# Filler matmuls ahead of the first weights in eight blocks instead of one, and a newly laid out issue table

## The chip, the core and the metric

The kernel runs on one core of one Trainium2 chip. A core has five engines that run side by side, each through its own list in order, and wait for one another by semaphores: TensorE (PE in the profile; PEld are its weight loads), VectorE (DVE), ScalarE (ACT), GpSimd (POOL) and SyncE (SP). SP here does nothing but issue DMAs; a few are issued by ACT. The metric is the device time of one execution in microseconds (us), median of the runs.

## The reference, cut to what matters

One block of a transformer with conditioning, on 2048 tokens of 512 features (bf16):

```python
mod = silu(c) @ w_mod                      # six rows of 512: sa, ca, ga, sb, cb, gb
h = layernorm(x) * (1 + ca) + sa
x = x + ga * A(h)                          # attention over 8 tokens, spaced by 2, 32 heads of 16
h = layernorm(x) * (1 + cb) + sb
x = x + gb * B(h)                          # second layernorm, then an MLP over the tokens
```

A: `qkv = h @ wqkv`; each token attends to itself and to the tokens 2, 4, ... 14 before it; then `@ wo`. B mixes tokens, not features: `gelu(h.T @ w1 + b1) @ w2 + b2` with w1 of 2048 x 1792 and w2 of 1792 x 2048.

## The kernel before, in words

The 2048 tokens are 16 tiles of 128. `SIZES=(2, 4, 4, 4, 2)` groups the tiles into five chunks, and `build_chunk(ch)` adds the work of one chunk to a graph. Names in the table carry the chunk or the tile.

Of one chunk: `ln1s`, `ln1v`, `rstd1`, `rste1`, `nb1`, `n1` are the first layernorm of its tiles (statistics, variance, an Ln and an Exp on ACT, the norm). `tr` transposes the normed tiles on PE and `hT` evicts them with the scale `a1col`; for chunks 2 to 4, `xt` does the transposing by DMA. `qkv{ch}_{t}{j}` are the projections (t: 0 q, 1 k, 2 v), `ev` their evictions from PSUM. `halo_v` copies the last 16 tokens of the chunk before, `vd` are four DMAs that lay v out anew. `qk` (VectorE, four of 128x4096 a chunk, or 128x2048 in the short chunks 0 and 4) multiplies q by the shifted k's, `red` sums the products over the head on PE; `max`, `sub`, `exp`, `esum`, `rcp`, `rcq`, `smB` are the softmax; the four `a2` DMAs lay its weights out for `pv` (VectorE, as large as `qk`), whose products `pvacc` sums on PE and `oev` evicts. `wo` is the output projection, `x1` adds the result to x, `ln2*` and `ln3*` are the layernorms of B with `n2`, `aff`, `afb`, `h3`. Chunks 0 and 1 use the raw weights, and the scale goes into `hT`; the others use weights that `wsc` has scaled.

The MLP: `mlp1_{layer}_{ft}_{tile}` are the first matmuls over those token tiles that are normed already, `park` and `padd` hold partial sums, `gelu` closes them; `mlp2_{tile}` are fourteen matmuls of 512 columns for each output tile, `fin` and `st_out` finish and store.

The opening: `ld_c`, then `cps` (a tiny matmul that transposes c), `silu_exp`, `silu_dve`; `modcols1` and `modcols0` are 16 small matmuls each on the loads `ld_wmod1` and `ld_wmod0`, and give `a1col` (1 + ca) and `sab` (sa). `qvb0` and `qvb1` project sa through the raw weights. `warm` blocks are fillers: matmuls of 512 columns on the identity into a PSUM buffer that nobody reads.

What sets the order: nothing is moved at run time. `ORDER` (line 180) is one list of all operations. `_Graph.schedule` (line 87) walks it, checks that everything an operation needs stands ahead of it, picks the engine, and gives out ring buffers (six PSUM banks, four product buffers `big`, five `vd` buffers) in that order; each engine's list is the table's order. A suffix picks the engine where several can do the work (`:a` ACT, `:d` VectorE, `:p` GpSimd, none the first one named in the code); `:s` skips, and `:q` splits a matmul into four of 32 columns of weights. SP's DMAs are such a list too: a DMA that waits holds all behind it.

In the old table PE's list opens `cps tr0_0 warm0 modcols1 modcols0 tr1_2 tr1_0 qvb0 qkv0_00 qkv0_02 qkv0_10`. `warm0` has 12 matmuls, and the key `wmA1` makes both `modcols` wait for it (lines 538 and 553); `warm1` (2) stands at the end of the table, and the other six are skipped. All instructions have one line number in the profile, that of a helper, so rows are told apart by their tiles: psS<-ident is a filler, psS<-sc,big is `modcols`, psS<-ident,h a transpose, psS<-sab,wst is `qvb0`, psS<-hT,wst are projections, big<-q_sb,k_f is `qk`, big<-a2sb,vD is `pv`, lsb<-lsb,rb is `smB`, hT<-h on SP is `xt`.

Of the kernel before, what the change touches and what calls it, by code (L numbers as in the profile page):

```python
# [42 lines left out]
class _Graph:  # L43
# [7 lines left out]
    def add(self, eng, dur, fn, **kw):  # L51
        return self.add_any([(eng, dur, fn)], **kw)
# [103 lines left out]
def _ap(base, dims):  # L156
    return bass.AP(base.tensor, base.offset, [list(base.ap[0])] + [list(d) for d in dims])
# [23 lines left out]
halo0 ident ld_c act_table cps silu_exp ld_x1 ld_x0 ln1s0 ln1v0 ln1s1:a ln1v1 rstd1_0 rste1_0 ld_x_2_8 ld_x_1_2 nb1_0  # L181
consts ln1s9 silu_dve n1_1 n1_0:p tr0_0 ln1s8 ld_x_1_4 ln1s4:a ld_x_2_6 ln1s3:a warm0 ln1s5 ln1s7 ld_wmod1 ln1v5
ld_wmod0 modcols1 modcols0 ln1v9 ln1v8 ln1v4 ln1s2 ln1v2 ld_wqkv0 ln1v7 ln1v3 ln1s6 ln1v6 rstd1_1 rste1_1 nb1_1 n1_4:d
rstd1_2 rste1_2 n1_2:d n1_5:d nb1_2 ld_wqkv1 n1_3 n1_7 n1_6:d a1col hT0_2:d n1_9 tr1_2 tr1_0 hT1_1 wsc0_1:p hT0_1:d
sab hT0_0:d ld_x_3_12 hT0_3:d hT1_3:d qvb0 qvb_cp0 qkv0_00 warm6:s wsc1_3:a hT1_2:d qkv0_02 ev0_00 ld_wqkv2 qkv0_10
qkv0_12 ld_b2 ev0_10 ld_x_4_14 wsc1_2:p qkv0_20 wsc0_0 qvb1 ld_x_3_10 wsc0_3:p hT1_0:d ev0_02 wsc2_2:a ln1s13 ln1s12
ev0_12 ln1v12 ln1v13 wsc1_1:a qkv0_22 qk0_1 qkv1_13 ld_wmod2 ld_wo3 qk0_0 qk0_2 n1_8 red0_0 red0_1 ln1s11:a qkv1_03:q
qvb_cp1 qk0_3 xt6 red0_2 ld_wmod3 ev1_13 ev1_03 red0_3 mask wsc2_3:a ln1v11 ln1s10 ld_b1 ld_wo0 xt8 ev0_20 xt7 qkv1_11
ev1_11 ln1v10 max0 qkv1_01 ev1_01 rstd1_3 ev0_22 qk1_3 xt9 sub0 exp0 qkv1_00 ev1_00 qkv1_10 ev1_10 wsc1_0:a vd0_0
qk1_1 qkv1_02 esum0 rcp0 wsc0_2:p qk1_0 ev1_02 qkv1_12 qkv1_23 ld_wmod4 ld_wmod5 rcq0 ev1_12 qkv1_21 rste1_3 smB0  # L190
nb1_3 a2_0_0 ln1s15:a a2_0_2 qkv2_00 qk1_2 qkv2_10 n1_13:p red1_0 ev2_00 red1_1 ev2_10 red1_2 red1_3 ln1v15 a2_0_1
ev1_23 qkv2_13:q qk2_0 ev1_21 max1 modrow qkv1_20:q sub1:q ln1s14:a a2_0_3 pv0_0 wsc2_1:a halo_v1:a qkv1_22:q mrows
vd0_3 vd0_1 vd0_2 ld_wo1 ev2_13 pv0_3 pvacc0_0 n1_10 exp1 ev1_20 ld_row0 qkv2_02:q pv0_1 pv0_2 warm3:s ld_wo2 esum1:q
rcp1 ev1_22 rcq1 smB1 qkv2_03 ev2_03 pvacc0_1 pvacc0_2 xt10 wsc2_0:a pvacc0_3 ev2_02 oev0_2 qkv2_01:q vd1_3 qkv2_12
oev0_0 ev2_01 ln1v14 qkv2_11 ev2_12 rstd1_4 qkv2_23:q n1_11 vd1_1 n1_12 a2_1_2 qkv2_22:q a2_1_3 qk2_3 woq_s rste1_4
wo1:q wo0:q ev2_11 a2_1_0 a2_1_1 vd1_2 x1_1 red2_0 qk2_2 nb1_4 qk2_1 ev2_22 qkv2_20 x1_0 ev2_23 ln2m0 biascols pv1_3
n1_14 xt13 xt12 ln2q0 ln2q1 n1_15 qkv2_21 red2_1 red2_2 ln2w0 red2_3 xt11 rstd2_0 pv1_1 ev2_21 rste2_0 qkv3_10:q
ev3_10 qkv3_02:q ev3_02 qkv3_00:q ev2_20 ev3_00 nb2_0 n2_1 n2_0 qkv3_11 max2 qkv3_01 ev3_01 sub2 pvacc1_1 oev1_1
halo_v2 ld_row2 vd1_0 pvacc1_3 pv1_2 qkv3_12:q ld_row1 exp2 aff0 ev3_12 qkv3_13:q halo_v3:a ev3_11 pv1_0 esum2
pvacc1_2 rcp2 oev1_3 oev1_2 afb0 pvacc1_0 oev1_0 rcq2 xt14 ld_w1_0_0 ld_w1_0_512 vd2_2 qkv3_03:q qk3_1 smB2 ln3s0:a  # L200
# [38 lines left out]
def kernel(  # L239
# [27 lines left out]
    WARM=(12, 2, 2, 2, 2, 2, 2, 2),  # L267
# [28 lines left out]
    def ps(slot):  # L296
        return psS[slot.i][:]
# [731 lines left out]
```

## Time and profile before

| | |
|---|---|
| median of 3 runs | 198.6 us (197.77 to 198.84) |
| span of the profiled execution, first to last instruction | 196.8 us |
| the profiled execution's own time | not listed apart from the three runs; the median is 1.8 us over the span |
| PE busy | 185.2 us (94%), 1850 matmuls |
| VectorE busy | 156.6 us (80%), 244 instructions |
| ScalarE busy | 124.9 us (63%), 293 instructions |
| GpSimd busy | 19.9 us (10%), 38 instructions |
| DMA | 35.95 MB, mean 183 GB/s |

How to read it: times of the profile count from the first instruction. A matmul's recorded length includes its way through the array, so two in a row overlap in the record, and the spacing of their starts is the better measure; for that reason a busy PE is not PE at its peak. Idle time of an engine that is not the one that holds up the others costs nothing.

### The profile page before, as it was taken

The page shows a single profiled execution, that of the slowest core. Times are in us where ns is not written, and L with a number is a line of the kernel's source. Part 1 is how long each engine was busy: PE and PEld are TensorE (multiplying, and loading weights), DVE is VectorE, ACT ScalarE, POOL GpSimd, SP SyncE. Part 2 cuts the span into 40 slices and gives each one's busy share as a digit, 9 for nine tenths or more (in the row PEclk, how much of TensorE's full clock was granted, in tenths as well). Part 3 has the DMA queues.
Part 4 walks back from the last instruction along what each step waited for, and adds up shares of the span by engine and source line. Part 5 has one row for each costly group of instructions (what it writes and reads, how often), then busy time and mean ns, then how long its engine had stood idle before and what let it go on. Part 6 is the DMA issues. An engine that isn't in the chain of part 4 may idle for free.

```text
span 196.8 us, 4628 instructions
## 1 busy us (share of the span) xinstructions
PE 185.2 (94%) x1850; PEld 95.5 (48%) x1867; DVE 156.6 (80%) x244; ACT 124.9 (63%) x293; POOL 19.9 (10%) x38
## 2 busy tenths in 40 slices
PE   0699999999999999899999999999999999999994
PEld 0369554654444467244544454444444444444453
DVE  2888999999999999999999999965841633453664
ACT  6877999998999999999797889812760000000000
POOL 5123006320000005030000031200000000000000
PEclk9999999999999999999999999999999999999999
DMA  5998478778899732969674768888939293001112
GB/s 169 312 366 248 115 165 256 235 216 238 165 193 317 252 131 80 312 167 249 199 200 136 159 176 180 197 250 170 336 65 309 82 257 102 30 27 53 53 53 82
DMA packets 55369, 35.95 MB, mean 183 GB/s; under 512 B 24628, under 2 KB 52788, under 8 KB 55348
## 3 DMA queue, kind: packets, MB, share of 16 engines
q1 hardware_dynamic: 53468, 34.05, 63.2%
q10 hardware_dynamic: 1880, 1.61, 2.5%
q8 instruction: 14, 0.23, 0.5%
q14 instruction: 7, 0.06, 0.1%
HBM read 22.03 MB, written 2.10 MB: 123 GB/s over the span
## 4 chain that ended last, share of the span: by engine, by line
PE 73%; DVE 13%; ACT 5%; issue 3%; DMA 2%; SPq 1%; POOL 0%; DVEq 0%; ACTq 0%
PE psS L131 71%; DVE big L131 9%; DVE h L131 2%; PE psL L131 2%; ACT junk L131 1%; SPq L131 1%; DMA vD<-v_sb 1%; ACT xx L131 1%; DMA xx<-in_A_x_dram 1%; DVE m L131 1%; ACT o_sb L131 1%; ACT lsb L131 0%; DVE mv L131 0%; POOL h L131 0%; ACT v_sb L131 0%
## 5 line engine op out<-in xcount | busy, mean ns | idle before, releaser
L131 PEld LDWEIGHTS <-wst 128*128 128x128 bf16 (+1 forms) x566 | 35.5, 100 | 31.9 <-issue 1.3
L131 PE MATMUL psS<-h,wst 128*32 128x512 bf16 (+1 forms) x400 | 50.5, 379 | 0.4 <-issue 0.3
L131 DVE TENSOR_TENSOR big<-q_sb,k_f 128x4096 bf16<-128x4096 bf16 (+1 forms) x20 | 36.4, 1857 | 0.5 <-ACT k_f L131 0.5
L131 DVE TENSOR_TENSOR big<-a2sb,vD 128x4096 bf16<-128x4096 bf16 (+1 forms) x20 | 36.6, 1858 | 0.0
L131 DVE SCALAR_TENSOR_TENSOR h<-psS,bcol,rows_bc 128x512 f32<-128x512 f32 (+2 forms) x18 | 12.4, 690 | 24.2 <-PE psS L131 24.0
L131 PE MATMUL psS<-hT,w_qkv 128*32 128x512 bf16 (+3 forms) x414 | 28.7, 337 | 0.8 <-ACT v_sb L131 0.4
L131 PEld LDWEIGHTS <-w_qkv 128*32 128x32 bf16 (+1 forms) x462 | 19.9, 108 | 16.4 <-issue 2.7
L131 PE MATMUL psS<-gT,big 128*128 128x512 bf16 x109 | 24.3, 379 | 0.2
L131 POOL TENSOR_SCALAR h<-xx,rs,nb 128x512 bf16<-128x512 bf16 x6 | 10.6, 1777 | 84.2 <-DVE nb L131 84.2
L131 PEld LDWEIGHTS <-big 128*128 128x128 bf16 x144 | 12.0, 98 | 13.7 <-issue 0.5
L131 ACT ACTIVATE junk<-xx 128x512 bf16<-128x512 bf16 x28 | 17.7, 631 | 1.3 <-DVE xx L131 0.3
L131 ACT ACTIVATE h<-xx,nb,rs 128x512 bf16<-128x512 bf16 x22 | 17.2, 818 | 0.4 <-DVE nb L131 0.4
L131 PE MATMUL psS<-woq,o_sb 128*32 128x512 bf16 (+1 forms) x123 | 15.8, 380 | 0.4 <-ACT o_sb L131 0.4
L131 ACT ACTIVATE gT<-psS,bcol 128x512 bf16<-128x512 f32 x14 | 8.8, 686 | 10.6 <-DVE psS L131 10.6
L131 DVE TENSOR_TENSOR psS<-psS,gT 128x512 f32<-128x512 f32 x14 | 9.2, 695 | 6.3 <-PE psS L131 6.3
L131 DVE TENSOR_TENSOR h<-h,xx 128x512 bf16<-128x512 f32 (+2 forms) x18 | 11.4, 633 | 0.7
L131 ACT ACTIVATE q_sb<-psS,qvb 128x512 bf16<-128x512 f32 (+1 forms) x20 | 11.6, 603 | 0.3 <-PE psS L131 0.2
L131 PEld LDWEIGHTS <-group 128*32 128x32 bf16 x288 | 7.0, 96 | 9.8 <-issue 4.0
L131 PE MATMUL psS<-hT,wst 128*128 128x256 bf16 (+2 forms) x74 | 11.3, 333 | 0.1
L131 ACT ACTIVATE v_sb<-psS,qvb 128x512 bf16<-128x512 f32 (+1 forms) x20 | 11.2, 607 | 0.0
L131 DVE TENSOR_TENSOR h<-h,rows_bc 128x1024 bf16<-128x1024 bf16 (+2 forms) x14 | 10.5, 759 | 0.0
L131 ACT ACTIVATE k_f<-psS 128x512 bf16<-128x512 f32 x16 | 9.7, 606 | 1.1 <-PE psS L131 1.1
(90 smaller groups left out, 223.3 us busy)
## 6 DMA issues: line engine op xcount, KB each, us to landing
vD<-v_sb SPq DMA_DIRECT2D x12, 524.5 KB, 4.8
big<-in_B_w_dram SPq DMA_DIRECT2D x4, 896.0 KB, 7.5
vD<-v_sb SPq DMA_DIRECT2D x8, 268.5 KB, 3.1
wst<-in_B_w_dram SPq DMA_DIRECT2D x3, 640.0 KB, 5.4
xx<-in_A_x_dram SPq DMA_DIRECT2D x7, 256.0 KB, 5.6
wst<-in_B_w_dram SPq DMA_DIRECT2D x2, 800.0 KB, 4.7
gT<-in_w_mod_dram SPq DMA_DIRECT2D x3, 512.0 KB, 5.4
wst<-in_B_w_dram SPq DMA_DIRECT2D x2, 768.0 KB, 5.6
```

The lines of the kernel that those rows point to most:

```text
L131: r = fn(*a, **k)
```

## The change

The computation and the loads are the same. Three things differ.

1. The fillers: `WARM` gives eight blocks with 2, 12, 1, 1, 3, 1, 1 and 1 matmuls, and a new argument `GATE` names for five of them a token tile (1, 8, 2, 4, 6) as the moving operand in place of the identity; such a block reads the tile and so waits for its load. The old `wmA1` key, by which `modcols` waited for the filler, is gone.
2. The table is new as a whole. PE's list now opens `cps warm0 warm1 warm7 warm6 warm4 warm2 warm5 warm3 modcols1 tr0_0 tr1_0 tr1_2 modcols0 qkv0_00 qvb0 qkv0_10 qkv0_12 qkv0_02`. The first seventeen DMAs on SP keep their order; behind them it changes (in chunk 1: `vd1_2 xt13 xt11 a2_1_0 a2_1_3 a2_1_2 a2_1_1 xt12 vd1_0 vd1_3 ld_row2 vd1_1`; before: `vd1_3 vd1_1 a2_1_2 a2_1_3 a2_1_0 a2_1_1 vd1_2 xt13 xt12 xt11 ld_row2 vd1_0`).
3. The choice of engine changes for some operations. By count, old to new: `hT` on VectorE 7 to 3, on ACT 1 to 5; `wsc` on VectorE 1 to 3, ACT 7 to 4, GpSimd 4 to 5; `n1` on ACT 10 to 6, GpSimd 2 to 6; `n2` on VectorE 0 to 3, ACT 12 to 11, GpSimd 4 to 2; `h3` on VectorE 9 to 7, GpSimd 3 to 5; `halo_v` on ACT 3 to 1, GpSimd 1 to 3; `ln1s` on VectorE 10 to 9, `ln3s` 11 to 9, the rest on ACT; one `ev` and one more `x1` on VectorE; stores issued by SP 5 to 10; `:q` on 38 operations instead of 48.

```diff
-    WARM=(12, 2, 2, 2, 2, 2, 2, 2),
+    WARM=(2, 12, 1, 1, 3, 1, 1, 1),
+    GATE=(None, None, 1, 8, 2, 4, 6, None),
...
-        def f_warm(s_w=s_w, n_w=n_w):
+        g_w = GATE[w_]
+
+        def f_warm(s_w=s_w, n_w=n_w, g_w=g_w):
+            rhs = _ap(ident[:, 0:1], [[0, 4], [1, P]]) if g_w is None else xx[:, g_w, :]
             for _ in range(n_w):
-                nc.tensor.matmul(ps(s_w), lhsT=ident[:], rhs=_ap(ident[:, 0:1], [[0, 4], [1, P]]), start=True, stop=True)
-        if w_ == 0:
-            f_warm0, s_w0 = f_warm, s_w
-            continue
-        G.add_any([("pe", 0.216 * n_w, f_warm), ("skip", 0.0, lambda: None)], reads=["ident"], alloc=s_w, frees=s_w,
-                  name=f"warm{w_}")
+                nc.tensor.matmul(ps(s_w), lhsT=ident[:], rhs=rhs, start=True, stop=True)
+        G.add_any([("pe", 0.216 * n_w, f_warm), ("skip", 0.0, lambda: None)],
+                  reads=["ident"] + ([] if g_w is None else [("xx", g_w)]), alloc=s_w, frees=s_w, name=f"warm{w_}")
...
-    add("pe", 0.216 * WARM[0], f_warm0, after=[G.ops[-1]], alloc=s_w0, frees=s_w0, writes=["wmA1"], name="warm0")
...
-    add("pe", 0.42, lambda: f_cols(1), reads=["sc", ("wmodA", 1), "wmA1"], writes=["wmA1"], alloc=s_m[1], name="modcols1")
+    add("pe", 0.42, lambda: f_cols(1), reads=["sc", ("wmodA", 1)], alloc=s_m[1], name="modcols1")
...
-    add("pe", 0.42, lambda: f_cols(0), reads=["sc", ("wmodA", 0), "wmA1"], frees=s_wm, alloc=s_m[0], name="modcols0")
+    add("pe", 0.42, lambda: f_cols(0), reads=["sc", ("wmodA", 0)], frees=s_wm, alloc=s_m[0], name="modcols0")
```

The start of the new table, with the operations in which the fillers and the first projections stand:

```diff
+ld_c ident act_table cps silu_exp silu_dve ld_x1 ld_x0 halo0 ld_x_2_8 warm0 ln1s1:a consts ld_x_1_2 ld_x_1_4 ln1s0
+ln1v1 ld_x_2_6 ld_wmod1 ld_wmod0 ln1v0 ld_wqkv0 warm1 warm7 warm6 warm4 ld_wqkv1 ln1s9 ln1v9 warm2 rstd1_0 ln1s8
+ld_x_3_12 ld_wqkv2 rste1_0 ln1v8 ln1s4:a ln1s5 warm5 ln1v5 nb1_0 ln1s2 ln1s3 ln1v4 ln1s7:a warm3 ln1v2 ln1v3 rstd1_1
+ln1s6 rste1_1 ln1v7 modcols1 nb1_1 ln1v6 n1_3:d n1_5 n1_0:p rstd1_2 n1_1:p n1_2:d tr0_0 rste1_2 n1_4:d a1col hT0_2
+tr1_0 hT0_1 tr1_2 hT0_3:d nb1_2 modcols0 n1_8:p ld_b2 hT0_0:d hT1_2 ld_x_4_14 n1_7:d hT1_3 wsc0_2 sab hT1_1:d qkv0_00
+qvb0 qkv0_10 qkv0_12 hT1_0 wsc0_1 qvb_cp0 ev0_10 ev0_00:d qkv0_02 qkv0_20 ld_x_3_10 ln1s13 qkv0_22 ln1s12:a ld_wmod2
```

More of the change, by code (lines that the diff above doesn't have):

```diff
@@ L180 @@
 ORDER = """
[L181 to L185, printed above, removed]
@@ L191 @@
[L191 to L195, printed above, removed]
@@ L196 @@
[L196 to L200, printed above, removed]
@@ new lines @@
+ln1v13 ev0_12 qkv1_13 ld_wo3 ev0_02 qk0_0 red0_0 qkv1_03:q wsc2_1 qk0_1 qk0_2 red0_1 red0_2 qk0_3 red0_3 wsc0_0:a
+ln1s11:a ln1v12 n1_6:p wsc0_3:p ln1v11 xt6 mask ln1s15 max0 qkv1_01 ld_b1 ev1_13 wsc1_3:p qkv1_11 n1_9 ld_wmod5 ev1_03
+sub0 wsc1_1:p qk1_3 ln1s10:a ld_wmod3 ev1_01 ln1v10 qvb1 qkv1_00 ev1_11 exp0 qkv1_10 qkv1_12 ev1_00 qvb_cp1 qk1_1
+ev0_22 ev1_10 esum0 ev1_12 ln1v15 xt9 qk1_0 ev0_20 qkv1_02 xt8 wsc1_2:p rstd1_3 qkv1_21 qkv1_23 rcp0 xt7 rste1_3 rcq0
+qkv2_00 ev1_02 smB0 wsc1_0:p qkv2_10 nb1_3 ln1s14:a ev2_00 qk1_2 ev2_10 ld_wmod4 red1_0 ln1v14 qk2_0 n1_13 red1_1
@@ new lines @@
+n1_10 vd0_2 qkv1_22:q red1_2 red1_3 max1 ld_wo2 a2_0_1 vd0_1 ev1_21 qkv1_20:q a2_0_2 a2_0_3 ev1_22 ev1_23 wsc2_3:a
+modrow ev1_20 mrows a2_0_0 sub1:q pv0_2 exp1 qkv2_12:q vd0_0 pv0_1 ld_wo1 pvacc0_2 vd0_3 qkv2_02 esum1 rstd1_4 pv0_3
+wsc2_2:a ev2_02 xt10 n1_11:p pv0_0 rcp1 rcq1 ld_wo0 rste1_4 biascols ev2_12 ld_row1 wsc2_0:a ld_row0 qkv2_01 red2_0
+qkv2_03:q halo_v1 ev2_01 smB1 n1_12 halo_v2 biascols_cp pvacc0_0 qkv2_11:q vd1_2 pvacc0_1 xt13 xt11 ev2_11 qk2_2
+a2_1_0 qkv2_13:q nb1_4 qkv2_21:q ev2_03 woq_s ev2_13 a2_1_3 pvacc0_3 qkv2_20 qkv2_22 qk2_1 oev0_0 qk2_3 oev0_2 a2_1_2
@@ new lines @@
+ev2_21 wo1 a2_1_1 pv1_2 wo0 red2_1 xt12 x1_1 vd1_0 ev2_20 ev2_22 red2_2 red2_3 x1_0 ln2q0 qkv2_23 ln2m0 ln2q1 max2
+ev2_23 qkv3_03 ev3_03 vd1_3 ln2w0 qkv3_13 rstd2_0 n1_15 ld_row2 sub2 rste2_0 qkv3_11 qkv3_00 pv1_0 exp2 vd1_1 esum2
+ev3_11 rcp2 nb2_0 vd2_2 n2_0 qkv3_10 ev3_00 ev3_13 pvacc1_2 pv1_3 n2_1 oev1_2 ev3_10 pv1_1 aff0 rcq2 qkv3_01:q
+qkv3_02:q ev3_02 smB2 afb0 ev3_01 qkv3_22:q pvacc1_3 n1_14:p pvacc1_1 pvacc1_0 xt14 qkv3_12 qk3_3 qkv3_21 oev1_1 qk3_0
+qk3_1 oev1_3 a2_2_2 oev1_0 vd2_1 ln3s1:a qkv3_20 xt15 ev3_22 wo4 ev3_12 a2_2_0 a2_2_1 wo3 wo2 wo5 qk3_2 ln3s0:a red3_0
```

72 lines of the change are left out of this document (33 added, 39 removed).

## The prediction

> **What bounds the kernel now.** I read the windows by stage first, with edges where one chunk's work ends. Columns: stretch, its length, then the busy time of PE, PEld, DVE, ACT and POOL.
>
> ```profile
> 24.30:41.50 17.20, 16.96 (x216) 9.18 (x217) 17.20 (x14) 16.68 (x39) 5.40 (x2) 1.00 0.76 209
> ...
> 61.00:81.20 20.20, 19.17 (x332) 10.92 (x333) 20.20 (x15) 19.66 (x51) 2.67 (x1) 1.00 0.66 203
> 81.20:101.90 20.70, 20.27 (x295) 9.95 (x297) 20.64 (x30) 19.50 (x53) 1.82 (x2) 1.00 0.75 200
> ...
> 126.70:193.60 66.90, 66.58 (x333) 31.80 (x338) 35.66 (x55) 10.10 (x15) 0.00 (x0) 1.00 0.49 136
> ```
>
> From 24.3 to 101.9 VectorE has no idle time to speak of (17.20 of 17.20, 20.20 of 20.20, 20.64 of 20.70); PE and ScalarE have a little. From 126.7 on VectorE is half idle and PE full. Where does the lead pass from one to the other? The chain that ended last shows it (start, length, what):
>
> ```profile
> 101.89 0.62 PE psS L131 x8
> ...
> 102.67 16.71 PE psS L131 x182
> ...
> 119.54 10.74 PE psS L131 x49
> ```
>
> The eight matmuls at 101.89 are `pvacc3_3`, which sums VectorE's last product of chunk 3 (`pv3_3`). Behind them the chain is PE alone until 190.7, 49 matmuls of 512 columns in 10.74 us, 0.219 us each. So the kernel is two runs in series: VectorE from its first product to `pv3_3`, then PE's remaining list. A later start of the first, or a hole in it, moves the end one for one. What sets the start is in the first 18 us:
>
> ```profile
> 2.20 0.18 PE L131 MATMUL psS<-ident,c_t 4*128 4x4 bf16 x1 [2.20 <-DMA c_t<-in_c_dram]
> ...
> 3.73 1.02 SPq L131 DMA_DIRECT2D big<-in_w_mod_dram  x2
> ...
> 4.80 1.55 SPq L131 DMA_DIRECT2D wst<-in_A_wqkv_dram  x2
> ...
> 6.47 1.03 PE L131 MATMUL psS<-ident,h 128*128 128x128 bf16 x8 [4.09 <-POOL h L131]
> ...
> 7.30 5.20 PE L131 MATMUL psS<-ident 128*128 128x512 bf16 x12
> ...
> 9.46 0.19 ACT L131 ACTIVATION_READ_ACCUMULATOR junk<-xx 128x1 f32 x1
> ...
> 10.11 0.30 ACT L131 ACTIVATE lv<-mv,epscol 128x4 f32<-128x4 f32 x1 [0.47 <-DVE mv L131]
> ...
> 10.86 1.05 DVE L131 TENSOR_SCALAR h<-xx,mv,rs 128x512 bf16<-128x512 bf16 x3
> ...
> 12.33 0.94 PE L131 MATMUL psS<-sc,big 128*128 128x1 bf16 x32
> ...
> 13.13 1.05 PE L131 MATMUL psS<-ident,h 128*128 128x128 bf16 x16
> ...
> 14.02 0.67 PE L131 MATMUL psS<-sab,wst 128*128 128x1 bf16 x16
> ...
> 14.55 3.66 PE L131 MATMUL psS<-hT,wst 128*128 128x256 bf16 x32
> ...
> 15.20 0.51 DVE L131 TENSOR_SCALAR w_qkv<-wst,a1col 128x512 bf16<-128x512 bf16 x1
> ...
> 17.38 0.60 ACT L131 ACTIVATE k_f<-psS 128x512 bf16<-128x512 f32 x1 [0.91 <-PE psS L131]
> ...
> 18.07 1.23 DVE L131 TENSOR_TENSOR big<-q_sb,k_f 128x2048 bf16<-128x2048 bf16 x1 [0.51 <-ACT k_f L131]
> ```
>
> The twelve matmuls at 7.30 are the filler `warm0`, about 0.42 us each, half the later pace. `modcols1` (12.33) is queued behind them. From issue to landing its weights took (last column, us):
>
> ```profile
> big<-in_w_mod_dram SPq DMA_DIRECT2D x2, 512.0 KB, 6.0
> wst<-in_A_wqkv_dram SPq DMA_DIRECT2D x1, 512.0 KB, 7.8
> wst<-in_A_wqkv_dram SPq DMA_DIRECT2D x1, 512.0 KB, 8.8
> ```
>
> So `ld_wmod1` (issued 3.73) had landed at 9.7, and the filler held PE 2.6 us longer. The two wqkv loads landed at 12.6 and 14.15 (issued 4.80 and about 5.35). SP's first seventeen issues keep their order, so I keep these landings.
>
> **The change part by part. Fillers.** The first fourteen start behind the matmul at 2.20 instead of 7.30: 14 x 0.42 = 5.9, to 8.3. In the old run the half pace lasted from 6.47 to about 12.3, 5.8 us of unbroken PE work; the same from 2.4 gives full pace near 8.2. The eight others, of which seven wait for a token tile (the latest, tile 6, was issued before `ld_wmod1` on the same queue), then take 8 x 0.22 = 1.8: `modcols1` at 10.1. It is not what comes last.
>
> **First product.** In the new order ScalarE's third statistics pair, tile 7, ends where the old one did, 9.65; the old run took 0.75 from the Ln at 10.11 to the norms at 10.86, and three norms take 1.05, so `tr1_0` starts at 9.65 + 0.75 + 1.05 = 11.45 (`modcols1`, `tr0_0` and `a1col` are through). Then PE's list by the rows' spacing: two transpose blocks 0.89 (13.13 to 14.02), `modcols0` 0.80, so `qkv0_00` starts at 13.1 (old 14.55; its weights landed at 12.6); 0.88 for it (3.50 for four), `qvb0` 0.53, `qkv0_10` at 14.55, after its load's landing. In the old run the third of the four blocks began at 16.30 (14.55 + 2 x 0.875) and its eviction at 17.38, 1.08 later; then 0.60 and 0.09 to the product. New: 14.55 + 1.08 + 0.69 = 16.3. VectorE's own queue ahead of it ends in `ev0_00` and `ln1s13` behind `qvb_cp0` (14.9), both near 0.69 by the next rows, so also at 16.3:
>
> ```profile
> L131 DVE TENSOR_TENSOR psS<-psS,gT 128x512 f32<-128x512 f32 x14 | 9.2, 695 | 6.3 <-PE psS L131 6.3
> L131 DVE TENSOR_SCALAR h<-h,mv,rs 128x512 bf16<-128x512 bf16 x3 | 1.1, 405 | 0.0
> ```
>
> The gain is 18.07 - 16.3 = 1.7; bounds 0 (some landing or norm binds as before) and 2.2 (only the wqkv landings bind: 14.15 + 1.08 + 0.69 = 15.9).
>
> **VectorE's work behind it** up to `pv3_3`: added `wsc2_1` (0.51) and an aggregate (0.1), removed `h3_3` (0.41): +0.2. Four `hT` evictions and a statistics that VectorE sheds, and the two scalings and the eviction that it takes on, lie ahead of the first product and are in the 16.3. `pv3_3` ends 1.5 earlier.
>
> **PE's list.** Between `qkv0_00` and `esum1` it is the same but for `qvb0`, so PE leads by 1.4 - 0.53 = 0.9 there. That is enough for VectorE's `smB1`: old `esum1` 39.41, `smB1` 41.45, so there were 2.0 between; new 38.5 against 40.3, 1.8.
>
> ```profile
> 39.41 0.63 PE L131 MATMUL psS<-lsb,ident 128*32 128x128 bf16 x32
> ```
>
> ```profile
> 30.82 0.42 DVE L131 TENSOR_TENSOR lsb<-lsb,rb 128x512 bf16<-128x512 bf16 x1
> ...
> 41.45 0.68 DVE L131 TENSOR_TENSOR lsb<-lsb,rb 128x1024 bf16<-128x1024 bf16 x1
> ...
> 50.06 2.28 DVE L131 TENSOR_TENSOR big<-a2sb,vD 128x4096 bf16<-128x4096 bf16 x1
> ```
>
> Behind `pvacc3_3` PE has one matmul fewer (the residual of tile 10, which VectorE now adds): -0.2. The last tiles' norms and the other moves of engine there I cost at nothing: what hides them is PE's own list, first-layer matmuls on older tiles that stand ahead of the readers; where a norm comes after its reader's turn, that cover is gone and every microsecond of it counts.
>
> **SP's queue in chunk 1** is where something else comes late. Old: four `a2_1` copies right behind `smB1`, three transposes behind them. New: `vd1_2`, `xt13`, `xt11`, the copies, `xt12`, then `vd1_0`.
>
> ```profile
> 38.59 2.37 SPq L131 DMA_TRANSPOSE hT<-h  x1
> ...
> 42.35 3.45 SPq L131 DMA_DIRECT2D a2sb<-lsb  x4
> ...
> 46.55 4.58 SPq L131 DMA_TRANSPOSE hT<-h  x3
> ```
>
> ```profile
> a2sb<-lsb SPq DMA_DIRECT2D x1, 64.0 KB, 2.1
> vD<-v_sb SPq DMA_DIRECT2D x1, 524.5 KB, 3.0
> vD<-v_sb SPq DMA_DIRECT2D x1, 524.5 KB, 4.6
> vD<-v_sb SPq DMA_DIRECT2D x1, 524.5 KB, 7.4
> ```
>
> `smB0` (old end 31.24) comes near 30.0 (1.7 less the 0.6 that was added). Behind it SP has eight issues of 0.63, `xt10` 2.37 and three more of 0.63: it is at `vd1_2` at 39.3. Then `vd1_2` 0.6, two transposes 2.0 and 1.25 (4.58 for three: a long first one), copies 2.7 to 3.45: the last starts near 45.6 and lands at 47.7, in time for `pv1_2` (50.06 - 1.5 = 48.6). `xt12` 2.0; `vd1_0` starts at 48.3 and lands 3.0 to 7.4 later, 51.3 to 55.7; `pv1_0` wants it at 52.0 (48.6, a product of 2.2, a maximum of 1.15). So it costs 0 to 3.7; a gain is excluded because VectorE is full. The 3.0 is the row of a load issued beside copies (nothing), the 4.6 of one with transposes at its side (0.9), the 7.4 of one beside weight loads; the place has copies and transposes, so I take the middle of the first two, +0.4.
>
> **GpSimd** gets `n1_11` and, behind it, `halo_v1`, for which `vd1_2` waits on SP with the whole queue behind.
>
> ```profile
> 31.42 4.91 POOL L131 TENSOR_SCALAR h<-xx,rs,nb 128x512 bf16<-128x512 bf16 x1 [15.17 <-DVE nb L131]
> ...
> 41.01 1.21 POOL L131 COPY v_sb<-v_sb 128x64 bf16<-128x64 bf16 x1 [4.68 <-ACT v_sb L131]
> ```
>
> By the old rows, 1.1 earlier, the norm ends at 35.2 and the halo at 36.4 (1.21) to 40.1 (4.91, the worst there is); SP arrives at 39.3. I take the first, its own row: nothing; the other adds 0.8. The Trainium skill, "SBUF — State Buffer", Who interferes with whom, says that a VectorE instruction with two SBUF inputs and a GpSimd one that reads SBUF exclude each other for a whole instruction. By that rule a halo would wait for one product, under 2.3, and cost nothing; the norm's 4.91 spans two products, so here the trace is worse than the rule.
>
> **Sum** from the profiled execution: -1.5 - 0.2 + 0.4 = -1.3, span 196.8 to 195.5. The 1.8 between that span and the median 198.6 stays: 197.3.
>
> **The rivals.** *SP's queue decides (slower).* `vd1_0` lands as in the worst row: 55.7 against 52.0, 3.7 late, 198.6 - 1.7 + 3.7 = 200.6. It decides once `vd1_0` lands after 54.7 (the gain of 1.7 and 1.0 more). For it: transposes and copies change places; against it: the 7.4 was measured beside weight loads that are not there yet at 48.
> *The opening gives half.* `a1col` now stands behind three norms, and the first product behind an eviction and a statistics; one of them 0.8 late leaves 198.2.
> *The change doesn't do what it says.* A gated filler leaves a hole, and full pace starts only 5.8 after dense work at 11.45: PE does 2.9 less in that time, 2 behind the old run at `esum1`; `smB1` is about 1.1 late, 199.7. Against it stand 5.9 us of ungated filler. The Trainium skill, "TensorE: Matmul & The Clock Gate", Part 1, says that the window is free-running, so that the count of slow matmuls varies from run to run; the trace has one run, which cannot show it.
> *All of the filler's hold comes back.* 2.6 and the 0.2: 195.8; against it, the norms at 11.45.
>
> **How the numbers follow.** Forecast 197.3 (own range 196.7 to 198.0) 0.45; SP's queue 0.22; half 0.18; late clock 0.06; all of it 0.09. Half a per cent, 1.0 us, is about what a measurement of this kernel tells from no change: under 197.6 is faster, over 199.6 slower. Faster: 0.33 of the forecast and 0.09, 0.42. Within: 0.12, 0.18 and 0.02, 0.32. Slower: 0.22 and 0.04, 0.26. From 196.2 to 200.4 leaves out some 0.06 below and 0.13 above.
>
> **What would show it.** Half-pace matmuls from 2.4 to about 8, none after 10; `modcols1` at 10.1; `qkv0_00` at 13.1; first product at 16.3; VectorE as full as before from there to 100.3; no idle time ahead of `pv1_0` beyond 0.4; PE alone from 100.4. It is wrong if the first product is later than 17.3, if VectorE shows over a microsecond of new idle time before `pv3_3`, or if PE has holes after it.

## The result, and the profile after

The changed kernel takes **199.09 us** (median of 17 executions, 198.72 to 199.80); the kernel before, run beside it, 198.38 (17 executions, 197.77 to 199.20). The ratio is 1.0041, 95% interval 1.003 to 1.0053: 0.4% slower, where 0.6% faster was forecast. The profiled execution has a span of 197.4 us (before 196.8).

The opening first: TensorE's timeline (start, length, what).

```profile
2.32 5.01 PE L131 MATMUL psS<-ident 128*128 128x512 bf16 x15
7.79 1.67 PE L131 MATMUL psS<-xx,ident 128*128 128x512 bf16 x7 [0.46 <-DMA xx<-in_A_x_dram]
10.42 0.55 PE L131 MATMUL psS<-sc,big 128*128 128x1 bf16 x16 [0.96 <-DMA big<-in_w_mod_dram]
...
13.30 1.03 PE L131 MATMUL psS<-hT,wst 128*128 128x256 bf16 x8 [0.38 <-DVE hT L131]
```

`modcols1` starts when its weights land, at 10.42 (before 12.33), and the first projection at 13.30 (14.55). VectorE's first product follows at 16.64 instead of 18.07: a lead of 1.43 between these two executions. From 24 to 102 VectorE is as full as ever, by the windows (stretch, length, busy time of PE, PEld, DVE, ACT, POOL):

```profile
24.00:42.00 18.00, 17.85 (x200) 9.41 (x202) 18.00 (x17) 17.14 (x40) 5.53 (x3) 1.00 0.74 210
42.00:62.00 20.00, 20.00 (x248) 10.17 (x240) 20.00 (x16) 17.55 (x38) 5.85 (x1) 1.00 0.58 175
62.00:84.00 22.00, 19.67 (x334) 11.56 (x327) 22.00 (x19) 20.88 (x54) 3.64 (x3) 1.00 0.76 228
84.00:102.00 18.00, 17.93 (x283) 9.24 (x284) 18.00 (x25) 17.57 (x47) 2.22 (x2) 1.00 0.49 156
```

And yet the lead is gone: `pv3_3`, the second of the two products in these rows, ends at 101.84 before,

```profile
97.35 4.49 DVE L131 TENSOR_TENSOR big<-a2sb,vD 128x4096 bf16<-128x4096 bf16 x2
```

and at 102.00 in the changed kernel:

```profile
97.51 4.49 DVE L131 TENSOR_TENSOR big<-a2sb,vD 128x4096 bf16<-128x4096 bf16 x2
```

Without a hole, VectorE needed 85.36 from its first product to `pv3_3` instead of 83.77. Its instructions are longer. Its timeline shows which:

```profile
16.64 1.31 DVE L131 TENSOR_TENSOR big<-q_sb,k_f 128x2048 bf16<-128x2048 bf16 x1
17.86 0.78 DVE L131 TENSOR_SCALAR w_qkv<-h,a1col 128x512 bf16<-128x512 bf16 x1
18.57 3.89 DVE L131 TENSOR_TENSOR big<-q_sb,k_f 128x2048 bf16<-128x2048 bf16 x3
...
33.47 2.72 DVE L131 TENSOR_TENSOR big<-q_sb,k_f 128x4096 bf16<-128x4096 bf16 x1
...
50.24 2.69 DVE L131 TENSOR_TENSOR big<-a2sb,vD 128x4096 bf16<-128x4096 bf16 x1
```

A product of 128x4096 took 2.28 or 2.29 throughout the kernel before; these two take 2.72 and 2.69. One of the three short ones (3.89 together, before 3.50) takes 1.62 instead of 1.22, and the scaling `wsc2_1` 0.78. In GpSimd's timeline an instruction ends 0.55 to 0.65 us behind the start of each:

```profile
15.51 4.75 POOL L131 TENSOR_SCALAR w_qkv<-wst,a1col 128x512 bf16<-128x512 bf16 x4
...
31.36 2.69 POOL L131 TENSOR_SCALAR h<-xx,rs,nb 128x512 bf16<-128x512 bf16 x1 [11.10 <-DVE nb L131]
...
44.95 5.85 POOL L131 TENSOR_SCALAR h<-xx,rs,nb 128x512 bf16<-128x512 bf16 x1 [5.26 <-DVE nb L131]
```

The four scalings end at 20.26, the third of them at 18.50 (the long product began at 19.70), the norm of tile 11 at 34.05, that of tile 14 at 50.80.

Behind `pv3_3` the chain that ended last is PE alone, as in the kernel before (start, length, what):

```profile
98.89 91.92 PE psS L131 x558
```

PE has no hole there, and the last output lands 94.10 after `pv3_3` (before 94.15). The end is another matter. The last store and its landing, before (span 196.8):

```profile
194.55 0.33 SPq L131 DMA_DIRECT2D out_dram<-h  x1
```

```profile
out_dram<-h SPq DMA_DIRECT2D x1, 32.0 KB, 1.4
```

and after (span 197.4):

```profile
194.64 0.34 ACTq L131 DMA_DIRECT2D out_dram<-h  x1
```

```profile
out_dram<-h ACTq DMA_DIRECT2D x1, 32.0 KB, 1.5
```

By the trace's exact marks the stretch from that landing to the end of the span is 0.85 before and 1.34 after. It holds semaphores and drains alone; GpSimd's drain is the late one. So the 0.6 of the two spans is: -1.43 (first product), +1.59 (VectorE to `pv3_3`), -0.05 (PE's list), +0.49 (the end).

### The profile page after: what moved, and what is told of

Its sections match the earlier page's. It is cut to its first block, busy times and chain, and to the rows that moved or that the text cites. A ratio compares the mean times of both kernels' runs of the same rounds, so it can differ in the third digit from the quotient of the medians.

```text
span 197.4 us, 4399 instructions
## 1 busy us (share of the span) xinstructions
PE 186.6 (95%) x1745; PEld 96.2 (49%) x1745; DVE 158.5 (80%) x244; ACT 124.7 (63%) x295; POOL 31.7 (16%) x45
## 4 chain that ended last, share of the span: by engine, by line
PE 62%; DVE 18%; DMA 8%; issue 4%; SPq 3%; ACT 3%; DVEq 0%
PE psS L131 60%; DVE big L131 12%; DMA wst<-in_A_wqkv_dram 4%; DVE h L131 3%; SPq L131 3%; DMA woq<-in_A_wo_dram 3%; PE psL L131 2%; DVE m L131 1%; DMA a2sb<-lsb 1%; ACT k_f L131 1%; DVE lsb L131 1%; ACT h L131 1%; DVE mv L131 1%; ACT w_qkv L131 0%; DVE st L131 0%
## 5 line engine op out<-in xcount | busy, mean ns | idle before, releaser
L131 DVE TENSOR_TENSOR big<-q_sb,k_f 128x4096 bf16<-128x4096 bf16 (+1 forms) x20 | 37.4, 1897 | 0.0
L131 PE MATMUL psS<-hT,w_qkv 128*32 128x256 bf16 (+2 forms) x396 | 29.0, 328 | 0.0
L131 POOL TENSOR_SCALAR h<-xx,rs,nb 128x512 bf16<-128x512 bf16 x8 | 15.3, 1923 | 63.7 <-DVE nb L131 34.6
L131 PE MATMUL psS<-gT,big 128*128 128x512 bf16 x112 | 24.8, 379 | 0.0
L131 ACT ACTIVATE junk<-xx 128x512 bf16<-128x512 bf16 x30 | 18.8, 627 | 2.1 <-DMA xx<-in_A_x_dram 1.5
L131 PE MATMUL psS<-woq,o_sb 128*128 128x512 bf16 x64 | 15.9, 379 | 0.0
L131 ACT ACTIVATE h<-xx,nb,rs 128x512 bf16<-128x512 bf16 x17 | 13.2, 809 | 0.5 <-DVE nb L131 0.5
L131 PE MATMUL psS<-big,group 128*32 128x512 bf16 (+1 forms) x160 | 9.8, 338 | 2.3 <-DVE big L131 2.3
L131 ACT ACTIVATE q_sb<-psS,qvb 128x512 bf16<-128x512 f32 (+1 forms) x18 | 10.5, 611 | 0.6 <-PE psS L131 0.5
```

Source lines behind the costliest of these rows:

```text
L131: r = fn(*a, **k)
```

## The experiments

**Theory A, turns:** a GpSimd instruction that is open beside VectorE's products takes its turn between two VectorE instructions, and the one behind waits. **Rival B:** VectorE's own reordered work eats the lead. **Theory H, the end:** the 0.49 comes from the length of GpSimd's list, not from the work moved. All runs in one table. "First" is the start of VectorE's first product, "between" the time from there to the end of `pv3_3`, "idle" what of it VectorE waited, "end" the stretch behind the last landing with GpSimd's records (its queue's included) in brackets; all of these from one profiled execution each. Then the median, and the ratio to the kernel before, which ran beside each group: its median was 198.55 beside e1 to e4, 198.46 beside e5 to e8, 198.17 beside e9 to e11 and 198.27 beside e12 and e13, so medians of different groups compare by their ratios.

| run | first | between | idle | end | median | ratio, interval |
|---|---|---|---|---|---|---|
| before | 18.07 | 83.77 | 0.2 | 0.85 (65) | 198.38 | |
| after | 16.64 | 85.36 | 0.0 | 1.34 (73) | 199.09 | 1.0041, 1.003 to 1.0053 |
| e1_norms | 16.33 | 86.50 | 1.8 | 1.22 (70) | 199.87 | 1.0065, 1.0044 to 1.0087 |
| e2_wsc | 16.88 | 85.53 | 1.2 | 1.32 (71) | 199.38 | 1.0048, 1.0026 to 1.007 |
| e3_opening | 18.86 | 83.83 | 0.2 | 0.84 (65) | 199.50 | 1.0026, 0.9999 to 1.0053 |
| e4_turns | 16.21 | 87.13 | 0.0 | 0.84 (81) | 200.23 | 1.0079, 1.0053 to 1.0106 |
| e5_filled | 17.36 | 83.93 | 0.2 | 0.85 (65) | 198.22 | 0.9994, 0.9973 to 1.0014 |
| e6_tail_after | 17.03 | 84.93 | 0.0 | 0.84 (81) | 198.72 | 1.0023, 1.0006 to 1.0039 |
| e7_tail_before | 17.09 | 83.75 | 0.2 | 1.32 (73) | 198.69 | 1.0012, 0.9989 to 1.0036 |
| e8_noturns | 16.20 | 83.81 | 0.0 | 1.20 (72) | 198.00 | 0.9972, 0.9955 to 0.999 |
| e9_placed | 16.71 | 84.69 | 0.2 | 0.84 (81) | 197.79 | 0.9992, 0.9974 to 1.001 |
| e10_norms_dve | 16.67 | 87.02 | 1.8 | 1.20 (70) | 199.58 | 1.0092, 1.0064 to 1.0119 |
| e11_ungated | 17.34 | 84.85 | 0.0 | 1.34 (73) | 199.52 | 1.0073, 1.0046 to 1.0101 |
| e12_own | 16.35 | 84.85 | 0.0 | 0.91 (80) | 198.40 | 1.0004, 0.998 to 1.0028 |
| e13_best | 16.51 | 85.96 | 1.3 | 0.84 (80) | 198.16 | 0.9991, 0.9968 to 1.0014 |

### More turns, and none

Eight GpSimd instructions that nobody needs, behind `n1_14` in the table:

```diff
+    pj_b = T([P, 3 * P], BF, "pj_b")
+    for i_ in range(8):
+        add("pool", 0.8, lambda: nc.gpsimd.tensor_scalar(pj_b[:], _ap(ident[:, 0:1], [[0, 3], [1, P]]),
+            epscol[:, 0:1], 0.0, op0=ALU.mult, op1=ALU.add), reads=["ident"], writes=["pj_b"], name=f"pj_{i_}")
```

> The changed kernel with eight extra GpSimd instructions behind the norm of tile 14, each reading and writing 128x384 in SBUF (a constant scaled into a tile that nobody reads); no other engine waits for them. They are open from about 50.8 us on, while VectorE runs the products of chunks 1 and 3. Theory A (turns): each that gets its turn between two products adds 0.3 to 0.4 to VectorE; with boundaries that have no product behind them left out, four to eight of them count, so the last product of chunk 3 ends 1.2 to 3.3 later and the time is 200.3 to 202.4. Rival E (the three long products are no matter of GpSimd): nothing changes, 199.1, and no product of these chunks is longer than 2.3.

`pv3_3` ends at 103.34, 87.13 behind the first product. VectorE's timeline:

```profile
60.62 0.99 DVE L131 TENSOR_TENSOR h<-h,rows_bc 128x1024 bf16<-128x1024 bf16 x1
...
63.04 9.50 DVE L131 TENSOR_TENSOR big<-q_sb,k_f 128x4096 bf16<-128x4096 bf16 x4
...
72.53 2.60 DVE L131 TENSOR_TENSOR big<-a2sb,vD 128x4096 bf16<-128x4096 bf16 x1
```

Four products took 2.58 to 2.60 (two of them in the 9.50, which is 8.89 without turns) and two `aff`/`afb` 0.98 to 0.99 instead of 0.68: six turns of 0.30 to 0.32, some 1.85. From `smB1` to `pv3_3` the run is 1.85 longer than the changed kernel (61.34 and 59.49). Two of the eight were free; they ended while VectorE ran `max2`, which reads PSUM. Theory A holds, rival E falls. The median, 200.23, lies just under the 200.3 to 202.4 expected: the end is 0.5 shorter here (81 records).

Four instructions left out, with zeros written early in their places:

```diff
-wsc1_2:p
...
-wsc1_0:p
...
-n1_11:p
...
-n1_14:p
...
+consts n1_11 n1_14 wsc1_0 wsc1_2
...
+        if name in ("n1_11", "n1_14"):
+            add("pool", 0.1, lambda: nc.gpsimd.memset(dst, 0.0), writes=writes, name=name)
+            return
```

> The changed kernel without four of GpSimd's instructions that ran beside VectorE's products: the norms of tiles 11 and 14 and two of the weight scalings of chunk 2 and later (wsc1_0, wsc1_2) are left out, and GpSimd writes zeros in their places at 3 to 4 us instead. No other engine takes over their work, and all else is as in the changed kernel. Theory A (turns): the products that took 1.62, 2.72 and 2.69 us take 1.22, 2.28 and 2.28, VectorE's scaling 0.51 instead of 0.78, together 1.5; the last product of chunk 3 ends about 83.9 behind the first one (85.4 in the changed kernel), and the time is near 197.6. Rival B (the changed order of VectorE's own work eats the lead): it stays at 85.4 and 199.1. Rival J (something else takes the time over as soon as the turns are gone, as ScalarE did when it got the two norms): the products shorten, but VectorE shows idle time in their place.

```profile
17.44 0.34 DVE L131 TENSOR_SCALAR w_qkv<-h,a1col 128x512 bf16<-128x512 bf16 x1
17.70 3.48 DVE L131 TENSOR_TENSOR big<-q_sb,k_f 128x2048 bf16<-128x2048 bf16 x3
...
32.22 2.28 DVE L131 TENSOR_TENSOR big<-q_sb,k_f 128x4096 bf16<-128x4096 bf16 x1
...
48.55 2.28 DVE L131 TENSOR_TENSOR big<-a2sb,vD 128x4096 bf16<-128x4096 bf16 x1
```

The same four VectorE instructions without GpSimd beside them: 0.34 instead of 0.78, and 0.40, 0.44 and 0.41 less. 83.81 between, 83.9 expected, and 83.77 in the kernel before: VectorE's own reordered work costs 0.04, the turns are the rest of the 1.59. Rivals B and J fall. The median is 198.00 where 197.6 was expected; by the ratios (0.9972 against 1.0041) the four instructions are worth 0.69%, 1.4 us.

### Other engines in GpSimd's place

Two norms on ScalarE (e1), or on VectorE (e10, with the suffix `:d`), at their places in the table:

```diff
-n1_11:p
+n1_11
...
-n1_14:p
+n1_14
```

> The changed kernel with the norms of tiles 11 and 14 on ScalarE instead of GpSimd; nothing else. Theory A (turns): a GpSimd instruction that is open while VectorE's products run takes its turn between two of them, and the product behind it runs longer. In the changed kernel the product that began as the norm of tile 11 was ending took 2.72 us and the one at the end of the norm of tile 14 took 2.69, where products of their shape take 2.28. Both should fall to 2.28, VectorE's last product of chunk 3 should end 0.85 earlier (101.15 instead of 102.00) and the time should fall by about 0.8, to 198.3. Rival B (the changed order of VectorE's own work eats the lead): the two products may shorten, but the last product stays near 102.0 and the time at 199.1.

> The changed kernel with the norms of tiles 11 and 14 on VectorE itself instead of GpSimd. Theory A (turns): the two products fall from 2.72 and 2.69 to 2.28, but VectorE pays two norms of about 0.41, which is what GpSimd's turns cost it: the last product of chunk 3 ends as far behind the first as in the changed kernel (85.4, within 0.2), and the time is 199.1. So the help of GpSimd in these places is worth nothing. Rival (GpSimd takes work off VectorE's path): 0.8 slower, 199.9.

In e1 both products took 2.28, as A expects, but the time rose to 199.87: the 0.85 turned into waits for SP. `pv0_3` waited 0.97 for a `vd0` load and the first product of chunk 2's `pv` 0.83 for an `a2` copy. In e10 the second wait shows why. VectorE's timeline:

```profile
63.00 0.41 DVE L131 TENSOR_SCALAR h<-xx,mv,rs 128x512 bf16<-128x512 bf16 x1
...
73.17 2.29 DVE L131 TENSOR_TENSOR big<-a2sb,vD 128x4096 bf16<-128x4096 bf16 x1 [0.88 <-DMA a2sb<-lsb]
```

At the table's place the norm of tile 14 comes at 63.00, 12 us after GpSimd's; SP's `xt14`, in order, waits for it, and the copies stand behind `xt14`. So both expectations on the time failed (199.87 for 198.3 in e1, 199.58 for 199.1 in e10), and neither run could price a turn against an instruction of VectorE's own. e12 does, with each instruction at the place where GpSimd's copy was open:

```diff
-wsc1_2:p
...
-wsc1_0:p
...
-n1_11:p
...
-n1_14:p
...
+qk0_3 wsc1_2 wsc1_0
...
+nb1_3 n1_11:d
...
+nb1_4 n1_14:d
```

> The changed kernel with the norms of tiles 11 and 14 and the scalings wsc1_0 and wsc1_2 on VectorE itself, each where GpSimd's copy of them was open, so that the transpositions behind the norms are issued no later; and twelve early writes by GpSimd, so that it has 81 records and the end is that of the kernel before. Theory A (turns): GpSimd's turns cost VectorE 0.40, 0.44, 0.44 and 0.41, 1.7 in all; the four instructions on VectorE cost twice 0.33 (as the norms took in the run with them on VectorE) and twice 0.26 (a scaling without a turn in it), 1.2 in all. So the last product of chunk 3 ends 84.9 behind the first instead of 85.4, no product is longer than 2.3, and with the 0.5 of the end the time is 198.1. Rival (GpSimd takes work off VectorE's path): 86.5 behind the first, and 199.8.

84.85 between, 84.9 expected; no product over 2.32. In the changed kernel's profile GpSimd's help at these places cost VectorE 1.7; doing the work itself costs 1.0 (84.85 against e8's 83.81). The gain is not that large in every execution: in e6 and e11, below, one of the four costly turns is missing, and the same GpSimd work gives 84.93 and 84.85. The median is 198.40 (198.1 expected); in its profile PE's part behind `pv3_3` is 0.57 longer than in the changed kernel, since TensorE waits there once, 0.39 at 120.89, for a weight load (`wst`).

And three scalings on ScalarE:

```diff
-wsc2_1
...
+wsc2_1:a
...
-wsc1_2:p
+wsc1_2:a
...
-wsc1_0:p
+wsc1_0:a
```

> The changed kernel with three weight scalings taken from where the first products run: wsc1_2 and wsc1_0 from GpSimd to ScalarE, and wsc2_1 from VectorE to ScalarE (where the kernel before had it). Theory A (turns): the second of chunk 0's products falls from 1.62 to 1.22 us, the first from 1.31 to 1.22, and VectorE's scaling (0.78, of which 0.27 is waiting for GpSimd's turn) is gone: together 1.3 at most. ScalarE takes on three times 0.65, so I expect 1.0 of it at the last product of chunk 3 (101.0) and a time near 198.1. Rival B (only VectorE's own extra instructions count): 0.5 less, 198.6. Rival C (ScalarE is late with evictions instead): no change, or slower than 199.1.

The second product fell to 1.21 (the first stayed at 1.30), and `max0` ended 6.32 behind the start of the first product instead of 7.28, the 1.0 of theory A. Then ScalarE was late, as rival C said: VectorE waits 0.6 for a `k_f` eviction at 33.9 and 0.3 for `rb` at 42.2, with four shorter waits 1.2 in all. 199.38.

### Turns put where they are free

`wsc1_0` and `wsc1_2` read `a1x`, the norm of tile 11 reads `nbx`, its shift column alone:

```diff
+    add("dve", 0.15, lambda: nc.vector.tensor_copy(a1x[:], a1col[:]), reads=["a1col"], writes=["a1x"], name="a1x")
...
-qk0_2 qk0_3
+qk0_2 a1x qk0_3
...
-ln1v14 qk2_0
+ln1v14 nbx qk2_0
...
-nb1_4 woq_s qk2_1 qk2_3 pv1_2
+woq_s qk2_1 qk2_3 nb1_4 pv1_2
```

> The changed kernel with all its work, and three edits to when GpSimd may start: the scalings wsc1_2 and wsc1_0 read a copy of the scale column that VectorE makes behind the second product of chunk 0, the norm of tile 11 reads a shift column that VectorE makes just ahead of chunk 2's first product, and the shift column of tile 14 stands right ahead of pv1_2 instead of two products earlier; and the eight early writes by GpSimd from the run on the end of the span (81 records). Theory A (turns): GpSimd's instructions are then open during a product behind which VectorE reads PSUM, so their turns cost nothing: the products that took 1.62, 2.72 and 2.69 us take 1.22, 2.28 and 2.28, the scaling on VectorE 0.34, and the last product of chunk 3 ends 84.0 behind the first (83.8 without these four instructions, plus two column operations of 0.07 each). With the end at 0.85 the time is 199.1 - 1.4 - 0.5 = 197.2. Rival J (the waits move somewhere else): 198.5, as the end alone gives.

```profile
20.73 2.27 POOL L131 TENSOR_SCALAR w_qkv<-wst,a1x 128x512 bf16<-128x512 bf16 x2 [3.78 <-DVE a1x L131]
...
21.69 0.81 DVE L131 SCALAR_TENSOR_TENSOR mv<-mv,st 128x1 f32<-128x1 f32 x2
```

The norm of tile 14 cost nothing (both neighbours at their usual length), but the turn of one scaling hit a pair of column instructions (0.81 for 0.34; the first alone 0.65 for 0.21), which read SBUF too, and chunk 2's first product began 0.23 late for a `k_f` eviction. 84.69, so 0.7 of the 1.4 came back, and 197.79 instead of 197.2.

e13 joins what worked (three instructions on VectorE, tile 14's norm on GpSimd ahead of `max2`):

> As the run with the four instructions on VectorE, but the norm of tile 14 on GpSimd, opened right ahead of pv1_2 so that its turn falls where VectorE reads PSUM; 81 records of GpSimd. Theory A (turns): 0.33 less than with that norm on VectorE, 84.5 behind the first product and 197.7. Rival J (the waits move somewhere else): 198.1 or more, with idle time on VectorE.

Its profile has the wait for a `vd0` load again, the largest of all:

```profile
40.38 2.40 DVE L131 TENSOR_TENSOR big<-a2sb,vD 128x2048 bf16<-128x2048 bf16 x2 [1.34 <-DMA vD<-v_sb]
```

Less that, 84.6 (84.5 expected). Its median is 198.16 (197.7 expected). The load was issued at 35.5 to 35.9 in e1, e10 and e13 as in the changed kernel, where it was in time; why it lands late in some executions stays open.

### The end

Eight early writes, in the changed kernel (e6) and in the kernel before (e7):

```diff
+    pj_b = T([P, 1], F32, "pj_b")
+    for i_ in range(8):
+        add("pool", 0.1, lambda: nc.gpsimd.memset(pj_b[:], 0.0), writes=["pj_b"], name=f"pj_{i_}")
```

> The changed kernel with eight extra writes of one constant column by GpSimd at 3.5 to 4.5 us, where nobody waits for GpSimd. They change only the count of GpSimd's instructions: from 73 to 81 records. Between the last landing of an output and the end of the span lay 0.85 us in the kernel before (65 records) and 1.34 in the changed one, with GpSimd's last drain 0.5 late; it was 0.84 in the run with eight extra turns (81 records). Theory H (the end depends on where GpSimd's list of instructions ends): 0.85 again, so 0.5 less, 198.6. Rival I (the end is late because of the work that the change moved): 1.3 as before and 199.1.

> The kernel before with the same eight extra writes by GpSimd at the start: 73 records instead of 65, as many as the changed kernel has. Theory H (the end depends on where GpSimd's list of instructions ends): the stretch from the last landing to the end of the span grows from 0.85 to about 1.3 us, and the time from 198.4 to 198.9. Rival I (the end is late because of the work that the change moved): 0.85 and 198.4.

e6: 0.84, e7: 1.32, as theory H has it, and the table has no exception: 65, 80 and 81 records end in 0.84 to 0.91, 70 to 73 in 1.20 to 1.34, whatever kernel they belong to. Rival I falls. What in the list makes the end late no view shows. The times agree but do not show it: e6's ratio is 1.0023 against the changed kernel's 1.0041, and their intervals overlap; e7's, 1.0012, holds 1 in its interval.

e6 shows one thing more. Its list is the changed kernel's, but the norm of tile 11 (31.76) got its turn one product later, ahead of `max1`, and cost nothing:

```profile
31.76 4.87 POOL L131 TENSOR_SCALAR h<-xx,rs,nb 128x512 bf16<-128x512 bf16 x1 [11.12 <-ACT q_sb L131]
```

84.93 between, 0.43 less than in the changed kernel's profile. This is also what the 4.91 of the old norm was: it ended at 36.33, while VectorE read PSUM for `max1` (35.77, 1.21 long). A statistics instruction, which reads one operand from SBUF, does not wait either: in the changed kernel two `h3` norms of GpSimd end at 85.47 and 86.22, during statistics of the usual 0.66 to 0.69.

### The opening by itself

The change's fillers in the old table (e3):

```diff
-cps
+cps warm0 warm1 warm7
...
-ld_x_2_6
+ld_x_2_6 warm6 warm4 warm2 warm5 warm3
```

> The kernel before with the opening's fillers of the change and nothing else: the filling matmuls in eight blocks at the front of TensorE's list, five of them gated by a token tile, and the modulation columns no longer behind the block of twelve. Every other engine's list, and GpSimd's work, as before. Theory A (the lead is real and was lost to GpSimd's turns): the columns come at 9.7 to 10.5 instead of 12.33, VectorE's first product at 16.6 to 17.3 instead of 18.07, and with the old table nothing takes that lead away: the last product of chunk 3 ends near 100.9 and the time is near 197.5, about 1 below the kernel before. Rival D (the opening's lead is not worth anything further on, whatever GpSimd does): 198.4, as before.

Windows of e3 (the column behind POOL is the granted clock):

```profile
10.00:12.00 2.00, 0.88 (x25) 0.66 (x21) 1.90 (x7) 1.37 (x6) 0.00 (x0) 1.00 1.09 383
12.00:14.00 2.00, 1.65 (x33) 1.55 (x33) 1.97 (x10) 2.00 (x4) 0.99 (x2) 0.87 1.10 349
14.00:16.00 2.00, 2.00 (x12) 1.35 (x11) 2.00 (x6) 1.18 (x3) 1.75 (x3) 0.50 1.10 346
```

PE is idle more than half of 10 to 12, the clock falls to 0.50, and the first product comes at 18.86, later than ever. Nine of twelve executions had a mean clock of 0.989 to 0.991 and 199.2 to 199.9 us, three 0.998 or 0.999 and 197.7 to 198.1. The 83.83 between is that of the old table, so a lead would have been kept.

With two and three more matmuls behind the two column groups (e5):

```diff
-modcols1 modcols0
+modcols1 warm8 modcols0 warm9
```

> The kernel before with the change's opening (as in the run of the opening alone) and five more filling matmuls in the holes that its profile showed on TensorE: two between the two groups of modulation columns and three behind them, none gated. In the run without them TensorE was busy 0.88 of the 2.00 us from 10 to 12, the granted clock was 0.50 from 14 to 16 and the first product came at 18.86, and 9 of 12 executions had a mean clock near 0.991 and 199.2 to 199.9 us, the other three 0.998 and 197.7 to 198.1. Theory F (the holes let the clock fall): with the holes filled the granted clock stays at 1.00, all executions are of the second kind, the first product comes near 16.9, the last product of chunk 3 at 100.7 (83.8 behind it, as in the kernel before) and the median is near 197.8, 0.6 under the kernel before. Rival G (the clock falls for another reason): two kinds of executions as before, median 199.5.

The clock stays at 1.00 in all windows behind the opening's half pace, and its mean at 0.999 or over in all twelve executions: theory F holds. But the first product comes at 17.36, not 16.9, and the time, 198.22 where 197.8 was expected, is that of the kernel before (0.9994, 0.9973 to 1.0014). VectorE's timeline says why:

```profile
12.35 0.15 DVE L131 TENSOR_SCALAR a1col<-psS 128x4 f32<-128x4 f32 x1
```

The columns were ready at 10.47, and VectorE reaches `a1col` at 12.35, behind its statistics and norms. So in the old table VectorE's own queue covers most of what the filler holds up.

And the changed kernel without its five gated blocks (e11):

```diff
-warm6 warm4
+warm6:s warm4:s
...
-warm2
+warm2:s
...
-warm5
+warm5:s
...
-warm3
+warm3:s
```

> The changed kernel without the five filling blocks that wait for a token tile (eight matmuls between about 7.8 and 9.4 us); the fifteen ungated ones at the front stay. Theory F (holes let the clock fall): TensorE has little to do from about 7.3 to 10 us, the granted clock falls to about half for some microseconds behind it in part or all of the executions, and those are 1 to 2 us slower (200 to 201), with a mean clock near 0.99. Rival K (the gated blocks do nothing, since the clock that counts is that from 12 us on): 199.1 and no stretch at half the clock behind 12 us.

```profile
10.00:12.00 2.00, 1.53 (x28) 1.19 (x24) 1.49 (x8) 1.74 (x6) 0.00 (x0) 0.90 1.08 384
12.00:14.00 2.00, 2.00 (x30) 1.82 (x29) 1.54 (x5) 1.33 (x4) 0.96 (x2) 0.50 1.11 352
```

Seven of eleven executions had a mean clock of 0.991 or less, and in the profile it is 0.50 from 12 to 14. None of the changed kernel's 17 is under 0.996; of the runs that keep the gated blocks, e2, e9, e12 and e13 have one, two, one and one such execution in twelve. So the gated blocks hold the clock in most executions, not in all, and rival K falls. The loss is below the 1 to 2 expected, and not clear of noise: the ratio is 1.0073 against the changed kernel's 1.0041, and the intervals overlap. The first product came 0.7 later (17.34), and so one more of the scalings had its turn ahead of it; that gave 0.5 back.

## Why the prediction was wrong, step by step

- **The opening**: right, a little late. `modcols1` at 10.42 (10.1 forecast), first projection 13.30 (13.1), first product 16.64 (16.3): the load of the columns landed at 10.4 and not at 9.7 as before. Half pace ended early: by the spacing of the fillers (0.43, then 0.22) at 5.6 where 8.2 was forecast, and in the other profiles with this opening between 5.5 and 8.2. In this profile none came back behind 10, as forecast.
- **The size of the lead**: it was taken against one execution of the kernel before. The same list of PE in e7 ran its filler in 4.12 instead of 5.20 (all twelve at half pace in the one, seven in the other),

```profile
7.25 4.12 PE L131 MATMUL psS<-ident 128*128 128x512 bf16 x12
```

  and had its first product at 17.09 instead of 18.07. Against 16.64 the lead is 1.4 from the one and 0.45 from the other, and the ten profiles with the changed opening have their first product at 16.20 to 17.03. So the 1.43 of the two profiles, close to the 1.7 forecast, is partly luck. The Trainium skill, "TensorE: Matmul & The Clock Gate", Part 1, which the prediction cited without being able to show it, agrees: the number of slow matmuls of one list varies between runs.
- **VectorE's work behind the first product, priced at +0.2: the step that failed.** It was +1.59. The moved instructions themselves are worth 0.04 (e8: 83.81 against 83.77); GpSimd's four turns are worth 1.55 by that run, 1.7 by the lengths (0.44, 0.40, 0.44, 0.41). The prediction did weigh GpSimd against VectorE, but only for what GpSimd would wait. It never asked what VectorE waits, and its sum has no term for GpSimd's work on VectorE's path: GpSimd has six norms instead of two and five scalings instead of four, and with the earlier first product and the new places two norms and two scalings got a costly turn, where none did before. The Trainium skill, "SBUF — State Buffer", Who interferes with whom, says that the two exclude each other, in either direction. By that rule each of GpSimd's instructions under the products would have been a price, not a free move; the runs bear it out for a turn ahead of a product, at 0.40 to 0.44 each, and show turns at no price ahead of a PSUM read.
- **PE's list**: -0.2 forecast, -0.05 measured; PE has no hole behind `pv3_3`, as forecast.
- **SP's queue in chunk 1, +0.4**: nothing. VectorE is busy 20.00 of 20.00 from 42 to 62, so `vd1_0` was in time; in e8, without the turns, too (0.02 of idle time to `pv3_3`). The rival that put 3.7 on it did not happen. The load of this queue that does come late, in three of the runs, is one of `vd0`.
- **GpSimd's halos at nothing**: right; none shows on SP or VectorE.
- **The end**: not in the sum. "The 1.8 stays" holds between span and median (199.09 - 197.4 = 1.7), but the span itself has 0.49 more behind the last landing.

By the forecast's terms: -1.5 became +0.16, -0.2 became -0.05, +0.4 became 0, and 0.49 was missing; -1.3 became +0.60. It had said that it would be wrong if VectorE showed new idle time. It showed none: the lost time was booked as busy. The turns are not all of the miss: without the four of them the kernel is 0.28% faster than the kernel before (e8), not 0.6%, and what is still missing there is the end and the size of the lead.

## What to carry to other kernels

Where VectorE is the bound and reads two operands from SBUF, work given to GpSimd is not free. Here each of its large instructions cost VectorE 0.3 to 0.45 us, unless its turn fell ahead of a PSUM read or a statistics instruction; VectorE doing the work itself took 0.26 to 0.33. A full engine has no idle time to betray a loss: compare the lengths of equal instructions, not only the waits. And a lead read from one profile is one draw; take it from several executions if the opening contains fillers.

## What the runs showed of the hardware that was not expected

- A turn costs VectorE 0.30 to 0.32 for 128x384 and 0.40 to 0.44 for 128x512, less than GpSimd's instruction takes alone (0.58, and 0.69 to 0.77). A waiting instruction is not served at every boundary: the norm of tile 14 stayed open for 5.85 and let two products pass, and the same norm of tile 11 was served behind one product or behind two.
- Column instructions (128x1) that read SBUF wait as well (0.65 for 0.21 in e9). Statistics and reads of PSUM did not: they kept their 0.66 to 0.69 and 1.21.
- The span ends 0.3 to 0.5 later with 70 to 73 records in GpSimd's list than with 65, 80 or 81, in either kernel; eight early writes to one column switch it either way (e6, e7).
- Five fillers that fill about 1.5 us of holes decide whether the clock falls to 0.50 for some microseconds: without them the mean clock was low in nine of twelve executions (e3), with them in none (e5).
